# A gated, dilated convolution with fewer products: the next block's first product inside this block's slot, and plain rows moved to the front

## The chip, the cores and the metric

The kernel runs on one core of a Trainium2 chip. The metric is the device time of one execution in microseconds. Instructions run on five engines, each in its own order: TensorE (PE: matmuls; PEld: its weight loads), VectorE (DVE), ScalarE (ACT), GpSimd (POOL) and the sync engine (SP), from which nearly all transfers are issued. They wait for one another through semaphores.

## What is computed

Input x is [2, 16000, 256], w is [3, 256, 512] and w_o is [256, 256], all in bf16. The convolution has three taps, is causal, and has a dilation of two:

```
h[t] = x[t] @ w[0] + x[t-2] @ w[1] + x[t-4] @ w[2]     # 512 columns, zeros ahead of t = 0
z    = tanh(h[:, :256]) * sigmoid(h[:, 256:])
out  = z @ w_o
```

## The kernel before

**Groups.** The 32000 time steps are cut into groups. Fifteen *wide* groups hold 256 rows of 8 consecutive steps each. One of them (the eighth) holds rows of both batches, so its VectorE and GpSimd steps on x are two instructions instead of one. *Plain* groups hold rows of 4 steps: 128 rows at the start (`groups[0]`), 64 rows behind these (`extra`), and 128 rows at the end (`groups[-1]`). x is loaded with a transposing DMA (`load_wide`, L112, and `load_plain`, L98), channels on the 128 partitions; the first plain group is loaded as it is and turned on TensorE.

**Plain blocks.** A group has four blocks, one for each 128 of the 512 columns of h, in the order 0, 2, 1, 3, so that a tanh block is followed by its sigmoid block. A plain block multiplies each of the three taps by x (`direct`, L290 to L307). Tap 1 needs two operands, since its phases come from different rows.

**Wide blocks.** A wide block computes the eight phases with 14 matmuls of 128x512 instead of 24. It needs sums and differences of x, made once per group: `qs` in two halves (`wide_pairs`, "pairs", L217), `qp` (`wide_p`, "p", L223), `qm` in two halves (`wide_m`, "m", L226) and `qd` in two halves (`wide_d`, "d", L236). VectorE makes all of them but one half of `qd`, which GpSimd makes in two slices. Each of these tiles has two buffers, so a group writes into those of two groups back. It also needs six combinations of the weights; two of them, wt and wu, are made on TensorE with identity matrices (`weight_mm`, L171) and copied by ScalarE.

A block B has a PSUM tile `y` of two banks (three buffers; an output pool `o_ps` has two of one bank). Its steps, with T = TensorE, A = ScalarE, V = VectorE, G = GpSimd:

1. `first` (T, 2 matmuls on `qp`) into bank 0; `keep_first` (A, L274) copies it times 4 to `st`
2. `second` (T, 2, on `qm`) adds to bank 0; `keep_second` (A, L278) copies it times 2 to `sv`; `other` (G, L281) makes the other half of `sv` as sv - st
3. `third` (T, 2, on `qm`) adds to bank 0, behind keep_second; `split_bank` (V, L284) makes bank 1 from bank 0 and st
4. `late(B, 0)` (T, 4, on `qs`) adds to both banks, behind split_bank; `rest` (V, L288) subtracts both banks from `sv`; `activate(B, "sv")` (A, L322) gives four phases
5. `late(B, 1)` (T, 4, on `qd`) adds to both banks, behind rest; `activate(B, "y")` (A, L324) gives the other four
6. after two blocks, `gate` (V, L329) multiplies tanh and sigmoid halves; after four, the group's eight *pieces* are projected: `out_mm` (T, 4 matmuls of 128x256, L353), `out_evict` (A, L396), and a store by SP for every two pieces

**The order.** Every engine's order is written out by hand. A *slot* k stands for block k of all (slots 4 to 63 are the wide blocks; a group's slots 0 to 3 are those of its blocks). In the loop before (L496 to L532), with B the slot's block and V the one before it, TensorE does

```
first(B)  late(V, 0)  second(B)  [a block of extra, L518]  two pieces  third(B)  late(V, 1)
```

ScalarE does keep_first(B), "y" of the block before V, keep_second(B), two evictions, "sv" of V. VectorE does the gate that is due (a group's slots 0 and 2), then the steps for the next group (`prep`, L472 to L483: slot 1 pairs and d, slot 2 p, slot 3 pairs and m, next group's slot 0 the second m), then rest(V) and split_bank(B). GpSimd does a slice of `qd` in a group's slots 1 and 3, then other(B), both behind the last of VectorE's steps of this slot (`after`, which keeps GpSimd's reads of SBUF behind VectorE's instructions with two SBUF inputs). The slot of the first wide block (L433 to L450) is written out ahead of the loop, with wt and wu between its products.

Behind the loop (L536 to L577) stand the last wide block's late products, the last plain group, six waiting pieces, and then the last wide group's eight pieces and the plain group's two, evicted by ScalarE and VectorE in turn and stored one by one or in twos.

Of the kernel before, what the change touches and what calls it, by code (L numbers as in the profile page):

```python
# [13 lines left out]
def kernel(  # L14
# [42 lines left out]
    for b in range(B):  # L57
        t, end = (4 * (P + RE) if b == 0 else 0), (T - 4 * P if b == B - 1 else T)
        while t < end:
            n = min(need, (end - t) // 8)  # L60
# [29 lines left out]


# [112 lines left out]
    def wide_new(G):  # L204
        if "q" not in G:
            G["q"] = q_pool.tile([P, 2, 2, 2, CT, RW], bf16, name="qs")
            G["qm"] = q_pool.tile([P, 2, 2, CT, RW], bf16, name="qm")
            G["qp"] = q_pool.tile([P, 2, CT, RW], bf16, name="qp")
            G["qd"] = q_pool.tile([P, 2, 2, CT, RW], bf16, name="qd")

    def wide_pairs(G, h):

        wide_new(G)
        for col, sl in G["cols"]:
# [3 lines left out]
                out=G["q"][:, h, :, :, :, sl].rearrange("p h q ct r -> p h (q ct) r"),  # L218
# [3 lines left out]
    def wide_p(G):  # L222
        return nc.vector.tensor_tensor(out=G["qp"][:], in0=G["q"][:, 0, 0], in1=G["q"][:, 0, 1], op=ALU.subtract)  # L223

    def wide_m(G, h):
        return nc.vector.tensor_tensor(out=G["qm"][:, h], in0=G["q"][:, h, 0], in1=G["q"][:, h, 1], op=ALU.add)  # L226

    def wide_d(G, h, qs, eng, behind=None):

        wide_new(G)  # L230
        j = slice(4 + 2 * h + qs.start, 4 + 2 * h + qs.stop)
        for col, sl in G["cols"]:
# [3 lines left out]
            ins = after(eng.tensor_tensor(out=G["qd"][:, h, qs, :, sl], in0=a, in1=s, op=ALU.subtract), behind)  # L236
# [9 lines left out]
    def mm(B, wmat, mv, bank, first=False):  # L246
        for ct in range(CT):
            nc.tensor.matmul(  # L248
                B.y[:, bank, :], lhsT=wmat[:, ct, B.osl], rhs=mv[:, :, ct, :],
                start=first and ct == 0, stop=ct == CT - 1, skip_group_check=True,  # L250
            )

    def first(B):
        B.y = new_y()
        mm(B, W["wmh"], B.G["qp"], 0, True)
# [34 lines left out]
    def direct(B, taps, out):  # L290

        xt, R = B.G["x"], B.R
        xp, yp, xc, yc = views(B.G)
        for tap in taps:
            if tap == 1:
# [4 lines left out]
            for h, mv in parts:  # L300
                to = out if h is None else out[:, 2 * h * R:2 * (h + 1) * R]
                for ct in range(CT):
                    nc.tensor.matmul(  # L303
                        to, lhsT=w_taps[tap][:, ct, B.osl], rhs=mv[:, :, ct, :],
                        start=tap == TAPS[0] and ct == 0, stop=tap == TAPS[-1] and ct == CT - 1,
# [22 lines left out]
    def gate(G, dts):  # L328
        return nc.vector.tensor_tensor(out=G["z"][:, dts], in0=G["th"][:, dts], in1=G["sg"][:, dts], op=ALU.mult)  # L329
# [46 lines left out]
    def out_evict(G, rb0, jp, on_dve, single=False):  # L376
        o_ps = G["o", rb0, jp]
        copy = nc.vector.tensor_copy if on_dve else nc.scalar.copy
        if jp is None:
# [5 lines left out]
            for j in range(4):  # L385
                nc.sync.dma_start(out=rows[j], in_=osb[(j % 2) * n:(j % 2 + 1) * n, j // 2, :])
# [15 lines left out]
    extras = [Block(extra, oi) for oi in range(4)]  # L402
    ND = 4
    NB = len(blocks) - 4
# [28 lines left out]
    first(blocks[ND])  # L433
    keep_first(blocks[ND])
    for k in range(2, ND):
        activate(blocks[k], bank(blocks[k], k))
    weight_mm("wt")
    second(blocks[ND])
    keep_second(blocks[ND])
    weight_copy("wt")  # L440
    weight_mm("wu")
    weight_copy("wu")
    third(blocks[ND])
    split_bank(blocks[ND])
    wide_d(G0, 0, slice(0, 1), nc.gpsimd, last)
    other(blocks[ND], last)
    wide_d(G0, 0, slice(1, 2), nc.gpsimd, last)
    last = wide_d(G0, 1, slice(0, 2), nc.vector)
    load_wide(loaded_wide)
    loaded_wide += 1  # L450


    todo, made, pend = [], [], []
    gate_at = {}

    def note_gates(B, k):

        if B.oi % 2 == 1:
            gate_at.setdefault(k + 1, []).append((B.G, slice(B.oi // 2, B.oi // 2 + 1)))

    def do_gates(k):
        ins = None
        for G, dts in gate_at.pop(k, []):
            ins = gate(G, dts)
            if dts.stop == NT:
                todo.extend(pieces(G))
        return ins

    gate_at[ND + 1] = [(groups[0], slice(0, 1)), (groups[0], slice(1, 2))]
    gate_at[ND + 5] = [(extra, slice(0, 2))]  # L470

    prep = {}  # L472
    for G in wides[1:]:
        k0 = 4 * G["g"]
        for at, step in (
            (-3, lambda G=G: wide_pairs(G, 0)),
            (-3, lambda G=G: wide_d(G, 1, slice(0, 2), nc.vector)),
            (-2, lambda G=G: wide_p(G)),
            (-1, lambda G=G: wide_pairs(G, 1)),
            (-1, lambda G=G: wide_m(G, 0)),  # L480
            (0, lambda G=G: wide_m(G, 1)),
        ):
            prep.setdefault(k0 + at, []).append(step)  # L483
# [11 lines left out]

    for k in range(ND + 1, NB):  # L496
        B, V = blocks[k], blocks[k - 1]
        first(B)
        keep_first(B)
        late(V, 0)  # L500
        for Y in pend:
            activate(Y, "y")
            note_gates(Y, k)
        last = do_gates(k) or last
        for step in prep.pop(k, []):
            last = step() or last
        rest(V)
        second(B)
        keep_second(B)
# [5 lines left out]
        if k <= ND + 4:  # L515
            E = extras[k - ND - 1]
# [91 lines left out]
```

## Time and profile before

| | |
|---|---|
| time, median of 3 runs (lowest to highest) | 273.63 us (273.53 to 274.45) |
| the profiled execution: its own time | 274.15 us |
| its span, first to last instruction | 272.1 us |
| granted TensorE clock, mean | 0.997 |
| busy: PE, DVE, ACT, POOL | 261.4, 226.6, 248.7, 107.6 us |
| matmuls recorded | 1463 |

The profile shows one execution. Its page gives for each engine the busy time, for groups of instructions their count, mean duration and the idle time ahead of them, and a chain followed back from the last instruction to what released each step. The trace answers finer questions: single instructions in order of time, and who waited for whom. Matmuls are pipelined: a matmul of 512 columns is recorded as 0.38 us long, but the next one starts 0.216 after it, and its recorded end is modelled. On ScalarE and VectorE too, the next instruction may start about 0.1 ahead of the recorded end of the one before. So the texts count from start to start.

### The profile page before, as it was taken

The numbers are of one execution on the slowest core, as the hardware profiler recorded it, in microseconds if no ns is written. First come the engines' busy times: TensorE is split into PE (matmuls) and PEld (weight loads), VectorE is DVE, ScalarE is ACT, GpSimd is POOL, SyncE is SP. The second block draws the span as 40 slices with busy tenths as digits, with TensorE's granted clock in tenths as the row PEclk, the third lists the DMA queues.
The fourth block names the chain that finished last, engine by engine and source line by source line (L and its number), as shares of the span: only waits on it lengthen the run. The fifth ranks groups of instructions, "written<-read, shape, count | busy, mean of one in ns | idle before, by whom it ended". The sixth has DMA issues, their size and how long they took to land.

```text
span 272.1 us, 4200 instructions
## 1 busy us (share of the span) xinstructions
PE 261.4 (96%) x1463; PEld 142.1 (52%) x1464; DVE 226.6 (83%) x260; ACT 248.7 (91%) x380; POOL 107.6 (40%) x100
## 2 busy tenths in 40 slices
PE   7698999999999999999999999999999999999993
PEld 3443545555555555555555555555555555555572
DVE  2877998998898898899889889888988988876634
ACT  3577889999999999999999999999999999999882
POOL 1045355335435533544543453454345345423100
PEclk9999999999999999999999999999999999999998
DMA  8959441471927349192653919264381923122125
GB/s 208 206 116 201 80 94 51 127 192 55 198 106 170 113 109 209 52 223 85 142 143 99 217 42 241 78 150 132 102 215 41 241 79 93 69 77 77 41 77 193
DMA packets 78612, 35.00 MB, mean 129 GB/s; under 512 B 68864, under 2 KB 70912, under 8 KB 78592
## 3 DMA queue, kind: packets, MB, share of 16 engines
q1 hardware_dynamic: 77776, 34.09, 49.5%
q10 hardware_dynamic: 816, 0.66, 0.7%
q8 instruction: 11, 0.18, 0.3%
q14 instruction: 9, 0.07, 0.1%
HBM read 1.18 MB, written 16.38 MB: 65 GB/s over the span
## 4 chain that ended last, share of the span: by engine, by line
PE 86%; DVE 6%; DMA 3%; ACT 2%; issue 1%; SPq 0%; DVEq 0%
PE y L248 64%; PE o_ps L353 18%; DMA xq<-in_x_dram 3%; PE y L303 2%; DVE sv L288 1%; DVE qs L217 1%; PE y L171 1%; DVE y L284 1%; ACT st L274 1%; PE y L353 1%; DVE qd L236 1%; ACT sv L278 1%; ACT thw L324 1%; DVE zw L329 1%; DVE qp L223 1%
## 5 line engine op out<-in xcount | busy, mean ns | idle before, releaser
L281 POOL TENSOR_TENSOR sv<-sv,st 128x512 f32<-128x512 f32 x60 | 76.4, 1274 | 81.2 <-ACT sv L278 75.4
L288 DVE TENSOR_TENSOR sv<-sv,y 128x1024 f32<-128x1024 f32 x60 | 72.6, 1211 | 5.7 <-PE y L248 4.2
L396 ACT CAST osb<-o_ps 128x512 bf16<-128x512 f32 x115 | 63.0, 614 | 1.4 <-PE o_ps L353 1.3
L248 PE MATMUL y<-qd,wd_sb 128*128 128x512 bf16 x240 | 61.5, 379 | 1.3 <-DVE sv L288 1.1
L284 DVE SCALAR_TENSOR_TENSOR y<-st,y 128x512 f32<-128x512 f32 x60 | 41.8, 696 | 24.9 <-PE y L248 24.8
L353 PE MATMUL o_ps<-wo_sb,zw 128*128 128x256 bf16 x464 | 60.3, 273 | 0.0
L236 POOL TENSOR_TENSOR qd<-xq 128x512 bf16<-128x512 bf16 (+2 forms) x32 | 31.5, 988 | 65.1 <-DVE qm L226 39.6
L353 PEld LDWEIGHTS <-zw 128*128 128x128 bf16 x480 | 47.0, 98 | 17.6 <-issue 0.2
L274 ACT ACTIVATE st<-y 128x512 f32<-128x512 f32 x60 | 35.9, 598 | 8.5 <-PE y L248 5.4
L329 DVE TENSOR_TENSOR zw<-thw,sgw 128x2048 bf16<-128x2048 bf16 x30 | 38.7, 1292 | 2.8 <-ACT sgw L324 2.8
L248 PEld LDWEIGHTS <-wd_sb 128*128 128x128 bf16 x240 | 23.2, 97 | 30.3 <-DVE sv L288 1.6
L248 PE MATMUL y<-qp,wmh_sb 128*128 128x512 bf16 x120 | 35.7, 379 | 2.1 <-DVE qp L223 2.1
L217 DVE TENSOR_TENSOR qs<-xq 128x2048 bf16<-128x2048 bf16 (+2 forms) x32 | 36.8, 1154 | 0.8 <-DMA xq<-in_x_dram 0.8
L278 ACT ACTIVATE sv<-y 128x512 f32<-128x512 f32 x60 | 36.2, 603 | 1.4 <-PE y L248 1.4
L248 PE MATMUL y<-qm,w_sb 128*128 128x512 bf16 x120 | 35.5, 377 | 0.7 <-ACT sv L278 0.4
L248 PE MATMUL y<-qs,wt_sb 128*128 128x512 bf16 x120 | 35.7, 379 | 0.4 <-DVE y L284 0.4
L248 PE MATMUL y<-qm,wph_sb 128*128 128x512 bf16 x120 | 35.7, 379 | 0.0
L248 PE MATMUL y<-qs,wu_sb 128*128 128x512 bf16 x120 | 35.7, 379 | 0.0
L322 ACT ACTIVATE thw<-sv 128x1024 bf16<-128x1024 f32 x30 | 32.9, 1096 | 1.2 <-DVE sv L288 1.1
L322 ACT ACTIVATE sgw<-sv 128x1024 bf16<-128x1024 f32 x30 | 32.9, 1097 | 0.1
L324 ACT ACTIVATE sgw<-y 128x1024 bf16<-128x1024 f32 x30 | 30.5, 1017 | 0.6 <-PE y L248 0.6
L324 ACT ACTIVATE thw<-y 128x1024 bf16<-128x1024 f32 x30 | 30.6, 1019 | 0.0
(61 smaller groups left out, 167.6 us busy)
## 6 DMA issues: line engine op xcount, KB each, us to landing
out_dram<-osb SPq DMA_DIRECT2D x57, 256.0 KB, 2.0
out_dram<-osb_end SPq DMA_DIRECT2D x6, 128.0 KB, 1.8
w_sb<-in_w_dram ACTq DMA_DIRECT2D x2, 256.0 KB, 4.4
out_dram<-osb SPq DMA_DIRECT2D x2, 224.0 KB, 2.3
osb<-in_x_dram SPq DMA_DIRECT2D x1, 256.0 KB, 3.0
w_sb<-in_w_dram SPq DMA_DIRECT2D x1, 256.0 KB, 4.5
xq<-in_x_dram SPq DMA_TRANSPOSE x16, 6.9
wo_sb<-in_w_o_dram ACTq DMA_DIRECT2D x1, 128.0 KB, 2.6
```

The costliest lines, as they stand in the source:

```text
L217: ins = nc.vector.tensor_tensor(out=G["q"][:, h, :, :, :, sl].rearrange("p h q ct r -> p h (q ct) r"), in0=s, in1=a, op=ALU.subtract if h ...
L248: nc.tensor.matmul(B.y[:, bank, :], lhsT=wmat[:, ct, B.osl], rhs=mv[:, :, ct, :], start=first and ct == 0, stop=ct == CT - 1, skip_group_c ...
L274: nc.scalar.mul(B.st[:], B.y[:, 0, :], 4.0)
L278: nc.scalar.mul(B.sv[:, 0], B.y[:, 0, :], 2.0)
L281: after(nc.gpsimd.tensor_tensor(out=B.sv[:, 1], in0=B.sv[:, 0], in1=B.st[:], op=ALU.subtract), behind)
L284: nc.vector.scalar_tensor_tensor(out=B.y[:, 1, :], in0=B.st[:], scalar=-0.5, in1=B.y[:, 0, :], op0=ALU.mult, op1=ALU.add)
L288: nc.vector.tensor_tensor(out=B.sv[:], in0=B.sv[:], in1=B.y[:], op=ALU.subtract)
L322: nc.scalar.activation(out=dst[:, 2:4, :], in_=B.sv[:], func=func, scale=0.5)
L324: nc.scalar.activation(out=dst[:, 0:2, :], in_=B.y[:], func=func, scale=0.5)
L329: return nc.vector.tensor_tensor(out=G["z"][:, dts], in0=G["th"][:, dts], in1=G["sg"][:, dts], op=ALU.mult)
L353: nc.tensor.matmul(o_ps[:, q, :], lhsT=z_columns(G, rb0, jp, q, dt), rhs=wo_sb[:, dt, :], start=(dt == 0), stop=(dt == NT - 1),)
L396: copy(out=G["osb"][:, 2 * h:2 * h + 2, :], in_=o_ps)
```

## The change

Five things change.

- **Order in a slot.** The next block N's first product is made in this block's slot, one of its two matmuls ahead of third and one behind it, and keep_first(N) follows. TensorE's order becomes late(V, 0), second(B), two pieces, first(N) matmul 0, third(B), first(N) matmul 1, late(V, 1).
- **Other engines' orders.** VectorE's steps are in two lists, `small` (d, p, m and the gates of the front tiles) done first, and `big` (pairs and gates) behind them. So d comes ahead of pairs, p and m ahead of the gate, and m ahead of pairs. ScalarE's "sv" comes ahead of keep_first(N). GpSimd's slice comes ahead of second(B) in the program. Pieces whose gate is done in a slot are projected from the next slot on.
- **Start.** The first wide block's slot is part of the loop. wt and wu are made on TensorE ahead of its first product.
- **Plain rows.** `extra` has 128 rows instead of 64 and its blocks run in slots 4 to 7, in slots 4 and 5 with two of their taps at the head of the slot; half of its gate is made by GpSimd. One piece instead of two is projected in these slots.
- **End.** The last plain group has 64 rows. Its x is loaded as rows of 8 steps that overlap by 4, so that each tap has one operand (`load_end`), and two blocks share a bank and an activation. The last group's pieces are evicted in twos by ScalarE and VectorE and stored two at a time with one DMA.

The tiles `q`, `qm`, `qp`, `qd` are now taken when they are first written. The diff, cut to its core:

```
-        t, end = (4 * (P + RE) if b == 0 else 0), (T - 4 * P if b == B - 1 else T)
+        t, stop = (4 * 2 * P if b == 0 else 0), (T - 4 * RE if b == B - 1 else T)
...
-    groups.append(dict(wide=False, b=B - 1, r0=T // 4 - P, R=P))
-    extra = dict(wide=False, b=0, r0=P, R=RE, g="e")
+    extra = dict(wide=False, b=0, r0=P, R=P, g="e")
+    end = dict(wide=False, b=B - 1, r0=T // 4 - RE, R=RE, g="z")
...
+    def load_end():
+        xe = end["x"] = xt_pool.tile([P, 8, CT, RE], bf16, name="xe")
+        rows = x[end["b"], 4 * (end["r0"] - 1):4 * (end["r0"] + RE), :].rearrange("(r j) c -> r (j c)", j=4)
+        src = bass.AP(tensor=rows.tensor, offset=rows.offset, ap=[[4 * D, RE], [1, 8 * D]])
+        nc.sync.dma_start_transpose(out=xe[:].rearrange("p j ct r -> p (j ct) r"), in_=src)
...
-    def first(B):
-        B.y = new_y()
-        mm(B, W["wmh"], B.G["qp"], 0, True)
+    def first(B, ct):
+        if ct == 0:
+            B.y = new_y()
+        nc.tensor.matmul(
+            B.y[:, 0, :], lhsT=W["wmh"][:, ct, B.osl], rhs=B.G["qp"][:, :, ct, :],
+            start=ct == 0, stop=ct == CT - 1, skip_group_check=True,
+        )
...
+            if B.G is end:
+                parts = [(None, xt[:, 4 - 2 * tap:8 - 2 * tap])]
...
+    weight_mm("wt")
     for k in range(2):
         activate(blocks[k], bank(blocks[k], k))
...
+    weight_mm("wu")
     for k in range(2, ND):
         activate(blocks[k], bank(blocks[k], k))
...
+    for ct in range(CT):
+        first(blocks[ND], ct)
     weight_copy("wt")
+    keep_first(blocks[ND])
     weight_copy("wu")
...
+    small[ND] = [lambda: wide_d(G0, 1, slice(0, 2), nc.vector)]
+    small[ND + 1] = [lambda: gates_of(groups[0], slice(0, 2))]
+    small[ND + 2] = [lambda: gates_of(extra, slice(0, 1))]
     for G in wides[1:]:
         k0 = 4 * G["g"]
-            (-3, lambda G=G: wide_pairs(G, 0)),
-            (-3, lambda G=G: wide_d(G, 1, slice(0, 2), nc.vector)),
-            (-2, lambda G=G: wide_p(G)),
-            (-1, lambda G=G: wide_pairs(G, 1)),
-            (-1, lambda G=G: wide_m(G, 0)),
-            (0, lambda G=G: wide_m(G, 1)),
+            (-3, big, lambda G=G: wide_pairs(G, 0)),
+            (-3 if G["n"] > 1 else -2, small, lambda G=G: wide_d(G, 1, slice(0, 2), nc.vector)),
+            (-2, small, lambda G=G: wide_p(G)),
+            (-1, big, lambda G=G: wide_pairs(G, 1)),
+            (-1, small, lambda G=G: wide_m(G, 0)),
+            (0, small, lambda G=G: wide_m(G, 1)),
...
+    for k in range(ND, NB):
+        B, V = blocks[k], (blocks[k - 1] if k > ND else None)
+        E, early = (extras[k - ND] if k < ND + 4 else None), k < ND + 2
+        if E:
+            E.y = ps_o.tile([P, BANK], f32, name="e_ps", tag="o_ps")
+            if early:
+                direct(E, TAPS[:2], E.y[:])
+        if V:
+            late(V, 0)
+        if k >= ND + 2:
+            Y = blocks[k - 2]
             activate(Y, "y")
             note_gates(Y, k)
+        last = do(small, k) or last
+        last = do(big, k) or last
+        if k == ND:
+            wide_d(G0, 0, slice(0, 1), nc.gpsimd, last)
+            wide_d(G0, 0, slice(1, 2), nc.gpsimd, last)
         at = (2, 3) if B.G["n"] == 0 else (1, 3)
         if B.oi in at and B.G["n"] + 1 < len(wides):
             q = at.index(B.oi)
             wide_d(wides[B.G["n"] + 1], 0, slice(q, q + 1), nc.gpsimd, last)
+        second(B)
+        keep_second(B)
+        if k == ND + 4:
+            after(gate(extra, slice(1, 2), nc.gpsimd), last)
+            ready.extend(pieces(extra))
         other(B, last)
+        if V:
+            rest(V)
+        if E:
+            direct(E, TAPS[2:] if early else TAPS, E.y[:])
+        project(1 if E else 2)
+        evict()
+        N = blocks[k + 1] if k + 1 < NB else None
+        if N:
+            first(N, 0)
         third(B)
         split_bank(B)
+        if V:
+            activate(V, "sv")
+        if N:
+            first(N, 1)
+            keep_first(N)
+        if E:
+            activate(E, E.y[:])
+        if V:
+            late(V, 1)
+        todo += ready
+        ready.clear()
...
     late(V, 0)
+    activate(Y, "y")
     rest(V)
+    do(big, NB)
+    project(2)
     evict()
+    ye = new_y()
...
     activate(V, "sv")
+    plain_ends(ACT.Tanh, 0)
     late(V, 1)
     activate(V, "y")
+    plain_ends(ACT.Sigmoid, 1)
...
+    gate_phases(slice(2, 4))
...
+    for n, ps in enumerate(left):
+        quad(ps, n % 2 == 1)
+        for i, piece in enumerate(ps):
+            out_evict(*piece, i == 1)
+        if n == 0:
+            gate(end, slice(0, 2))
+            gate_phases(slice(0, 2))
+    for piece in pieces(end):
+        out_mm(*piece)
+        out_evict(*piece, False)
+    todo = [[(G, rb0, jp) for jp in jps] for jps in ((1, 2), (0, 3)) for rb0 in range(0, RW, P)]
+    for n, ps in enumerate(todo):
+        quad(ps, n % 2 == 0)
+        quad_store(ps, nc.sync)
```

`plain_ends` multiplies two end blocks into one bank of `ye` and activates them together. `quad` makes two pieces, into the two banks of a `y` buffer or into two of `o_ps`; `quad_store` evicts one with ScalarE and one with VectorE and issues one store for both. `gate_phases` makes the last gate for half of the phases at a time.

More of the change, by code (lines that the diff above doesn't have):

```diff
@@ L402 @@
     extras = [Block(extra, oi) for oi in range(4)]
+    ends = [Block(end, oi) for oi in range(4)]
     ND = 4
-    NB = len(blocks) - 4
+    NB = len(blocks)
     def bank(B, i):
@@ L445, with do, gates_of @@
[L445 to L454, printed above, removed]
+    ready, todo, made = [], [], []
+    small, big = {}, {}
+    def do(steps, k):
+        ins = None
+        for step in steps.pop(k, []):
+            ins = step() or ins
+        return ins
+    def gates_of(G, dts):
+        if dts.stop == NT:
+            ready.extend(pieces(G))
+        return gate(G, dts)
@@ L456, in note_gates @@
     def note_gates(B, k):
         if B.oi % 2 == 1:
[L459 to L472, printed above, removed]
+            big.setdefault(k + 1, []).append(lambda: gates_of(B.G, slice(B.oi // 2, B.oi // 2 + 1)))
@@ L530 @@
                 loaded_wide += 1
[L531 to L546 removed]
+            elif "x" not in end:
+                load_end()
+    assert not small
+    Y, V = blocks[NB - 2:]
```

153 lines of the change are left out of this document (60 added, 93 removed).

## The prediction

> **What bounds the kernel now.** I read the page's first part, then its chain, then the chain in order of time, then the timeline of one slot. Columns of the first: busy us, share of the span, instructions.
>
> ```profile
> span 272.1 us, 4200 instructions
> PE 261.4 (96%) x1463; PEld 142.1 (52%) x1464; DVE 226.6 (83%) x260; ACT 248.7 (91%) x380; POOL 107.6 (40%) x100
> PE 86%; DVE 6%; DMA 3%; ACT 2%; issue 1%; SPq 0%; DVEq 0%
> ```
>
> TensorE is busy throughout, and 86% of the chain that ends last is its work. This work has to be done in any case; only its waits can go. The chain in order of time (start, length) repeats one pattern per slot:
>
> ```profile
> 125.12 0.87 PE o_ps L353 x8
> 125.99 3.10 PE y L248 x14
> ...
> 252.37 0.87 PE o_ps L353 x8
> ```
>
> From 125.12 to 252.37 are 32 slots, 3.977 us each. Whether TensorE waits in them the timeline shows (start, length, engine, line; brackets: idle before and its releaser):
>
> ```profile
> 141.16 0.60 ACT L278 ACTIVATE sv<-y 128x512 f32<-128x512 f32 x1
> 141.64 1.09 ACT L396 CAST osb<-o_ps 128x512 bf16<-128x512 f32 x2
> 141.82 0.59 PE L248 MATMUL y<-qm,w_sb 128*128 128x512 bf16 x2
> 142.04 1.28 POOL L281 TENSOR_TENSOR sv<-sv,st 128x512 f32<-128x512 f32 x1
> 142.58 1.10 ACT L322 ACTIVATE thw<-sv 128x1024 bf16<-128x1024 f32 x1
> 143.11 0.59 PE L248 MATMUL y<-qp,wmh_sb 128*128 128x512 bf16 x2
> 143.12 1.28 DVE L329 TENSOR_TENSOR zw<-thw,sgw 128x2048 bf16<-128x2048 bf16 x1
> 143.74 0.60 ACT L274 ACTIVATE st<-y 128x512 f32<-128x512 f32 x1
> 144.24 1.02 ACT L324 ACTIVATE thw<-y 128x1024 bf16<-128x1024 f32 x1
> 144.32 0.68 DVE L226 TENSOR_TENSOR qm<-qs 128x1024 bf16<-128x1024 bf16 x1
> 144.84 1.04 PE L353 MATMUL o_ps<-wo_sb,zw 128*128 128x256 bf16 x8
> 144.93 1.21 DVE L288 TENSOR_TENSOR sv<-sv,y 128x1024 f32<-128x1024 f32 x1
> 145.14 0.60 ACT L278 ACTIVATE sv<-y 128x512 f32<-128x512 f32 x1
> 145.79 0.59 PE L248 MATMUL y<-qm,w_sb 128*128 128x512 bf16 x2
> ```
>
> From the third product (141.82) to the projection (144.84) are 14 matmuls in 3.02 us, 0.2157 each; the projection's eight take 0.87 (chain). TensorE alone would need 3.89 us. The next third (145.79) starts 0.08 late: it waits for keep_second (L278, ends 145.74), which stands behind the "y" activation (L324) and keep_first (L274), which waited for the first product (143.11 + 0.59 = 143.70). So a ring closes in 3.97 us: first 0.59 + 0.04, keep_first 0.50, "y" 0.90, keep_second 0.60 + 0.05, third and late 1.29. **The ring sets the slot, 0.085 above TensorE's own work.** Over slots 11 to 63 that is 53 x 0.085 = 4.5 us, with 0.3 more where a group spans both batches: 4.8.
>
> TensorE's other waits lie in front:
>
> ```profile
> 5.11 5.40 PE L303 MATMUL y<-xt,w_sb 128*128 128x512 bf16 x32 [0.44 <-ACT xt L188]
> 12.56 0.61 PE L248 MATMUL y<-qp,wmh_sb 128*128 128x512 bf16 x2 [2.05 <-DVE qp L223]
> 17.57 0.59 PE L248 MATMUL y<-qs,wt_sb 128*128 128x512 bf16 x2 [0.42 <-DVE y L284]
> 22.34 1.04 PE L248 MATMUL y<-qd,wd_sb 128*128 128x512 bf16 x4 [1.14 <-DVE sv L288]
> 24.94 0.83 PE L303 MATMUL e_ps<-xte,w_sb 128*128 128x256 bf16 x8
> 25.90 0.59 PE L248 MATMUL y<-qm,w_sb 128*128 128x512 bf16 x2
> ```
>
> A bracket starts at a matmul's modelled end, 0.16 after its slot is free, so idle is bracket plus 0.16: 2.2, 0.58, 1.30. The e_ps group frees its slot at 25.60 (24.94 + 0.83 - 0.17) and third follows 0.3 later, behind keep_second; three times. With 0.9 of smaller ones up to 43 us: 5.9. All waits: about 10.8 (4.8, 5.9, and 0.1 at the end).
>
> **The change part by part.** Blocks, tiles and columns multiplied are the same: 64 plain rows move from the end to the front. So I compare TensorE's waits, and what follows its last product.
>
> *The slot.* Let T be the start of the second half of a first product (ct 1). New order: late(V,1) T+0.22 (ends 1.24), late(.,0) 1.08, second 1.94 (ends 2.53), projection 2.37, half a first 3.24, third 3.46, next T at 3.89. keep_second starts at 2.57 and ends at 3.17: third has 0.24 to spare, the ring is open. ScalarE's steps, start to start: keep_first 0.50, "y" 0.90, keep_second 0.48 (141.16 to 141.64), two evictions 0.94 (to 142.58), "sv" 0.96 where nothing holds the next one:
>
> ```profile
> 253.93 1.10 ACT L322 ACTIVATE thw<-sv 128x1024 bf16<-128x1024 f32 x1
> 254.89 1.06 ACT L324 ACTIVATE thw<-y 128x1024 bf16<-128x1024 f32 x1
> ```
>
> Sum 3.78 of 3.89: it keeps up, with 0.11 spare. This gains 0.085 where nothing else comes late. **Next in line is VectorE.** Its steps, and GpSimd's:
>
> ```profile
> 131.19 1.22 DVE L217 TENSOR_TENSOR qs<-xq 128x2048 bf16<-128x2048 bf16 x1
> 132.33 0.69 DVE L236 TENSOR_TENSOR qd<-xq 128x1024 bf16<-128x1024 bf16 x1
> 133.10 1.04 POOL L236 TENSOR_TENSOR qd<-xq 128x512 bf16<-128x512 bf16 x1 [1.86 <-DVE qd L236]
> 134.09 1.28 POOL L281 TENSOR_TENSOR sv<-sv,st 128x512 f32<-128x512 f32 x1
> ```
>
> Pairs (L217) cost 1.14 start to start, a gate 1.20 (143.12 to 144.32), m (144.32 to 144.93) 0.61, and so p and d (L236), of its size. split_bank follows third at T+0.20 and leaves VectorE free at T+0.80. Then come the slot's steps, and rest (1.21 until its end), for which late(V,1) waits at T+4.11. In a group's slots 0, 2 and 3 the steps are 1.75 to 1.81: rest ends at 3.82, 0.24 before late needs it. In a group's slot 1 the change puts d ahead of the pairs, where it stood behind them. d writes the qd buffer of two groups back (two buffers), which the late(V,1) of the last block of that group reads until T+1.24. So d starts at 1.28, pairs 1.89, rest 3.03 to 4.24, late(V,1) 4.29: **TensorE waits 0.18**, with ScalarE's "sv" behind the same rest.
>
> GpSimd's slice of qd follows the pairs and moves with them: 3.16 to 4.20, then other (0.99 after the slice's start) 4.15 to 5.42. In the group's slot 2 p wants to start at 4.76 and meets it. What that costs:
>
> ```profile
> 38.39 1.28 POOL L281 TENSOR_TENSOR sv<-sv,st 128x512 f32<-128x512 f32 x1
> 39.14 1.61 DVE L329 TENSOR_TENSOR zw<-thw,sgw 128x2048 bf16<-128x2048 bf16 x1
> ```
>
> Pairs of the same size, not overlapped, took 1.22. The gate at 143.12 overlapped GpSimd's other (142.04 + 1.28) by 0.20 and took 1.28; the one at 39.14 overlapped it by 0.53 and took 1.61. VectorE stands while GpSimd works, but for some 0.14. So p counts from 5.28, gate 5.89, rest 7.09 to 8.30; late(V,1), which TensorE reaches at 8.18, waits to 8.35: 0.17. I take 0.15, as slices and gates differ by a few hundredths. In the Trainium skill, "SBUF — State Buffer" (section Who interferes with whom) says that a VectorE instruction with two SBUF inputs and a GpSimd one that reads SBUF block each other fully; the two gates agree, save the 0.14.
>
> Of the 13 groups with d first, 12 lie in slots 11 to 63: 12 x 0.33 + 0.3 at the batch border = 4.3 us of waits, against 4.8. **Gain 0.5: the ring's gain is nearly all given back.**
>
> *Front.* The 12 matmuls of wt and wu (2.59 us) now run right behind the first group's 32, from 10.31, while VectorE makes qp (ready at 12.50): the wait of 2.2 is gone. If that cover failed (a PSUM buffer not free), 2.2 would be back. New waits, placed by the same rows: third of the first wide block behind the copy of wu 0.3, the next third behind its keep_second 0.2; that block's late(V,1) 1.35, because d follows qp, pairs and two m (12.4 + 1.14 + 3 x 0.61 = 15.4), then GpSimd makes two slices (to 17.4) and other (to 18.7) with gate and pairs held behind them, so rest ends at 21.2 where TensorE is ready at 19.9. Slots 8 and 10 have no projection, as pieces now wait for the next slot; TensorE's own work there is 3.02, ScalarE's 3.78 - 0.94 + 0.5 for a front tile's activation = 3.3, the old ring 3.97: bounds 0.3 and 0.95 each. Placed in order, with ScalarE late from the slots before, I get 0.9 and 0.65. Small ones 0.35. Sum 3.75 against 5.9: **gain 2.15**. The front plain tile grows from 80 to 144 rows, and holds the sync queue longer ahead of the second wide load:
>
> ```profile
> 8.29 1.27 SPq L98 DMA_TRANSPOSE xte<-in_x_dram  x1
> 19.34 1.22 DVE L217 TENSOR_TENSOR qs<-xq 128x2048 bf16<-128x2048 bf16 x1
> ```
>
> By rows 1.27 becomes 2.3 us. The pairs at 19.34 show no DMA wait; with my 18.8 for them, a wait up to 0.5 would be hidden by GpSimd's hold. One gate of the front tile moves to GpSimd, whose gates no row shows: bounds are nothing and 1.3 (other's size); I take the slice's 1.04, which lies inside slot 8's wait.
>
> *Tail.* Only half as much plain work covers the last activations. late(.,0) stands behind split_bank with no first between them: 0.1. The first leftover pair of pieces ends 1.04 after its start; VectorE evicts (0.61, a copy being as long as m) and makes the end tile's gate (half an m, 0.35 to 0.4): at 2.15 the end piece may start, and TensorE is there after two pairs, 1.75: 0.4. Before, 0.1: **loss 0.4**. One operand per tap makes fewer, wider matmuls of the same columns: bounds minus 0.1 and 0.1, taken as nothing. Behind TensorE's last product:
>
> ```profile
> 266.87 1.04 PE L353 MATMUL o_ps<-wo_sb,z 128*128 128x256 bf16 x8
> 268.30 0.68 DVE L390 CAST osb_end<-o_ps 128x512 bf16<-128x512 f32 x1
> 268.87 0.89 SPq L363 DMA_DIRECT2D out_dram<-osb_end  x2
> ```
>
> TensorE ends at 267.9, the last copy at 268.98, and the last of two stores in a row goes out some 0.4 later. The copies now lag as long (a pair in the y buffers before it holds VectorE up), but one store of both pieces leaves at once; its landing may be slower for twice the size. Between nothing and 0.4, taken as half: **gain 0.2.**
>
> Sum: 0.5 + 2.15 - 0.4 + 0.2 = 2.45, say 2.5. The profiled execution had a span of 272.1 and took 274.15; the median of the runs is 273.63, 0.5 less. The span goes to 269.6, the median to **271.1 us**.
>
> **The rivals.**
> 1. *d does not wait* (the earlier reader of qd is through when VectorE gets there). Then all slots run at 3.89 and 12 x 0.33 = 4.0 more is gained: 267.1. For it: all four slots fit on paper. Against: late(V,1) ends 0.44 after VectorE is free. Chance 0.20.
> 2. *Third still waits for keep_second*: ScalarE has 0.11 to spare per slot, and one late step closes the ring again. Then the 29 slots without a VectorE wait stay at 3.977: 2.5 more, 273.6, no change. Chance 0.12.
> 3. *Slower: GpSimd becomes the ring*, in each group's slots 2 and 0. In slot 3 the slice (2.67) and other (3.66 to 4.93) already end 0.24 past the next m; with the 0.14 this holds it 0.10, inside its spare 0.24. From 0.14 more on, each tenth costs TensorE a tenth in slot 0, and slot 2 pays it in full. If VectorE's instructions hold GpSimd in turn by the 0.27 between slice and other lengths, (0.27 - 0.14) + 0.27 = 0.40 per group, 4.8 in all: 275.9. Against: GpSimd's rows keep 1.04 and 1.28 when overlapped. Chance 0.10.
> 4. *VectorE stands for the whole overlap*, without the 0.14: 12 x 0.14 = 1.7 more, 272.8, no change. The two gates speak against it. Chance 0.06. This is what the page "SBUF — State Buffer" of the Trainium skill would give.
>
> **How the numbers follow.** The forecast has 0.52, with its own range 269.9 to 272.2 (waits of 0.05 a slot either way in the 24 slots that wait). A measurement of this kernel can tell about 0.5% from no change, 1.4 us: faster means under 272.3. Faster: 0.52 less 0.01, and 0.20: 0.71. Within: 0.12 + 0.06 + 0.01 = 0.19. Slower: 0.10. Eight in ten: from 266.5 (most of rival 1) to 273.8 (rival 4 and over half of rival 2).
>
> **What would show it.** Slots 0 and 3 of a group 3.89 apart, slots 1 and 2 about 0.15 longer. Among VectorE's waits, qd behind TensorE's y, 13 times, near 0.47; among TensorE's, y behind VectorE's sv some two dozen times. keep_second no longer ends a TensorE wait past slot 11. No wait for qp near 12.5. I am wrong if VectorE's d shows no wait (rival 1), if third still starts 0.05 after keep_second's end (rival 2), or if other ends over 0.3 past the next small step in slot 0 (rival 3).

## The result and the profile after

The kernel takes **275.06 us** (median of 6 runs, 274.83 to 276.01); the kernel before beside it 273.83 (273.53 to 274.45). The ratio is **1.0051** (95% interval 1.0032 to 1.0070): slower by half a per cent, where 271.1 us and "faster" were forecast. The same kernel run again with the last experiments gave 1.0037 (1.0024 to 1.0050). The profiled execution took 275.64 with a span of 273.6.

The page's first lines and its chain, as shown of before (busy us, share, instructions):

```profile
span 273.6 us, 4186 instructions
PE 262.9 (96%) x1456; PEld 142.7 (52%) x1456; DVE 232.2 (85%) x260; ACT 249.0 (91%) x377; POOL 108.6 (40%) x101
PE 89%; DVE 3%; ACT 2%; issue 1%; DMA 1%; DVEq 0%
```

TensorE's share of the chain rose and the time rose too, so these lines don't say where the time went. The chain in order of time does. Here are the projections of one group and a half:

```profile
126.41 0.87 PE o_ps L365 x8
...
130.30 0.87 PE o_ps L365 x8
...
134.20 0.87 PE o_ps L365 x8
...
138.28 0.87 PE o_ps L365 x8
...
142.37 0.87 PE o_ps L365 x8
...
146.26 0.87 PE o_ps L365 x8
```

The even 3.977 us of before have become 3.89, 3.90, 4.08, 4.09, 3.89. Inside the two long slots the timeline shows, in order, d, the pairs, rest, p, the gate and rest again, with GpSimd's two pieces among them:

```profile
132.94 0.70 DVE L241 TENSOR_TENSOR qd<-xq 128x1024 bf16<-128x1024 bf16 x1 [0.31 <-PE y L253]
133.56 1.22 DVE L223 TENSOR_TENSOR q<-xq 128x2048 bf16<-128x2048 bf16 x1
...
134.69 1.21 DVE L297 TENSOR_TENSOR sv<-sv,y 128x1024 f32<-128x1024 f32 x1
...
134.91 1.04 POOL L241 TENSOR_TENSOR qd<-xq 128x512 bf16<-128x512 bf16 x1 [2.51 <-PE o_ps L365]
...
135.56 0.38 PE L261 MATMUL y<-qp,wmh_sb 128*128 128x512 bf16 x1
...
135.91 1.27 POOL L290 TENSOR_TENSOR sv<-sv,st 128x512 f32<-128x512 f32 x1
...
135.96 1.02 PE L253 MATMUL y<-qd,wd_sb 128*128 128x512 bf16 x4
...
136.43 1.30 DVE L229 TENSOR_TENSOR qp<-q 128x1024 bf16<-128x1024 bf16 x1
...
138.79 1.21 DVE L297 TENSOR_TENSOR sv<-sv,y 128x1024 f32<-128x1024 f32 x1
...
139.63 0.38 PE L261 MATMUL y<-qp,wmh_sb 128*128 128x512 bf16 x1
...
140.05 1.02 PE L253 MATMUL y<-qd,wd_sb 128*128 128x512 bf16 x4
```

In the first of them d waits 0.31 for TensorE (its bracket), rest ends at 135.90, and the late products start at 135.96. The matmul ahead of them (135.56) freed its slot 0.216 later, so TensorE lost 0.18. In the next slot p (136.43) takes 1.30 instead of 0.69, beside GpSimd's other; rest ends at 140.00, late starts at 140.05, and TensorE lost 0.20.

The end is the other place. TensorE's last rows, the last copy, and the sync queue:

```profile
266.48 1.04 PE L365 MATMUL o_ps<-wo_sb,zw 128*128 128x256 bf16 x8
...
267.90 0.68 DVE L604 CAST osb_end<-o_ps 128x512 bf16<-128x512 f32 x1
```

```profile
265.01 1.27 SPq L398 DMA_DIRECT2D out_dram<-osb_odd  x2
266.38 3.30 SPq L612 DMA_DIRECT2D out_dram<-osb_end  x4
```

TensorE ends 0.4 us earlier than before and the last copy as well, yet the span is 1.5 longer. The page's DMA part has the first trace of the reason: the end's stores (`osb_end`) land 4.1 us after their issue, where those of before, of half the size, took 1.8. Of the end piece's stores (`osb_odd`, the piece of the 64-row group, which has no partner) the page gives no landing. The first line is of after, the other three of before:

```profile
out_dram<-osb_end SPq DMA_DIRECT2D x4, 256.0 KB, 4.1
```

```profile
out_dram<-osb_end SPq DMA_DIRECT2D x6, 128.0 KB, 1.8
out_dram<-osb_odd SPq DMA_DIRECT2D x4, 32.0 KB, 1.9
38.28 2.47 SPq L386 DMA_DIRECT2D out_dram<-osb_odd  x4
```

In the kernel before, the odd piece belonged to `extra`, in front, and left at 38.28 in four stores of 32 KB. The change gives the 64 rows to the end group, so the odd piece is now stored at 265.01, right ahead of the last four stores. It also rewrites these stores, an edit that the diff above leaves out:

```diff
-for j in range(4):
-    nc.sync.dma_start(out=rows[j], in_=osb[(j % 2) * n:(j % 2 + 1) * n, j // 2, :])
+for q in range(2):
+    nc.sync.dma_start(out=rows[2 * q:2 * q + 2], in_=osb[:, q, :])
```

Each store of before wrote one phase and had the 64 rows as its outermost dimension. Each store of after writes two phases, and these two are its outermost dimension.

I cut both profiled spans, and a second one of the changed kernel, into stretches, and took from each the columns that its matmuls have, at 0.2157 us for 512 (the forecast's figure). What is left is TensorE's waiting, and slower products where it had them. The profile of before has records of 11 of the 12 matmuls of wt and wu; all 12 are counted. Each cell: length, and what is left.

| stretch | before | after | after, again |
|---|---|---|---|
| start to first plain product | 5.11 | 5.38 | 5.38 |
| to third product of slot 10 | 36.94, 6.3 | 37.61, 4.6 | 37.08, 4.1 |
| to third product of slot 63 | 211.12, 5.3 | 211.45, 5.9 | 211.46, 5.9 |
| to the end of the last product's slot | 14.58, 0.35 | 12.91, 0.83 | 12.91, 0.83 |
| to the end of the span | 4.37 | 6.23 | 6.23 |
| span | 272.1 | 273.6 | 273.1 |

Front and tail came near the forecast. The slots lost 0.55 instead of gaining 0.5, and the last stretch lost 1.86 instead of gaining 0.2.

### The profile page after: what moved, and what is told of

It is laid out like the page before. It is cut to its first block, busy times and chain, and to the rows that moved or that the text cites. A ratio compares the mean times of both kernels' runs of the same rounds, so it can differ in the third digit from the quotient of the medians.

```text
span 273.6 us, 4186 instructions
## 1 busy us (share of the span) xinstructions
PE 262.9 (96%) x1456; PEld 142.7 (52%) x1456; DVE 232.2 (85%) x260; ACT 249.0 (91%) x377; POOL 108.6 (40%) x101
## 4 chain that ended last, share of the span: by engine, by line
PE 89%; DVE 3%; ACT 2%; issue 1%; DMA 1%; DVEq 0%
PE y L253 55%; PE o_ps L365 18%; PE y L261 9%; PE y L315 4%; PE e_ps L315 1%; DVE sv L297 1%; DMA osb<-in_x_dram 1%; PE y L178 1%; DVE qp L229 1%; PE y L365 1%; DVE y L293 1%; ACT sv L287 0%; ACT st L283 0%; ACT thw L334 0%; ACT wu_sb L184 0%
## 5 line engine op out<-in xcount | busy, mean ns | idle before, releaser
L409 ACT CAST osb<-o_ps 128x512 bf16<-128x512 f32 x113 | 60.6, 592 | 1.6 <-PE o_ps L365 1.6
L365 PE MATMUL o_ps<-wo_sb,zw 128*128 128x256 bf16 x456 | 59.1, 273 | 0.0
L261 PE MATMUL y<-qp,wmh_sb 128*128 128x512 bf16 x120 | 45.3, 379 | 0.7 <-ACT thw L336 0.7
L223 DVE TENSOR_TENSOR q<-xq 128x2048 bf16<-128x2048 bf16 (+2 forms) x32 | 36.7, 1152 | 1.3 <-DMA xq<-in_x_dram 1.3
L253 PE MATMUL y<-q,wu_sb 128*128 128x512 bf16 x120 | 35.7, 379 | 0.0
L253 PE MATMUL y<-q,wt_sb 128*128 128x512 bf16 x120 | 35.7, 379 | 0.0
L341 DVE TENSOR_TENSOR zw<-thw,sgw 128x2048 bf16<-128x2048 bf16 x29 | 35.2, 1215 | 0.0
L334 ACT ACTIVATE sgw<-sv 128x1024 bf16<-128x1024 f32 x30 | 32.0, 1068 | 2.8 <-DVE sv L297 1.7
L334 ACT ACTIVATE thw<-sv 128x1024 bf16<-128x1024 f32 x30 | 32.1, 1069 | 2.0 <-DVE sv L297 1.0
```

The costliest lines, as they stand in the source:

```text
L223: ins = nc.vector.tensor_tensor(out=sums(G, "q")[:, h, :, :, :, sl].rearrange("p h q ct r -> p h (q ct) r"), in0=s, in1=a, op=ALU.subtract ...
L253: nc.tensor.matmul(B.y[:, bank, :], lhsT=wmat[:, ct, B.osl], rhs=mv[:, :, ct, :], start=False, stop=ct == CT - 1, skip_group_check=True,)
L261: nc.tensor.matmul(B.y[:, 0, :], lhsT=W["wmh"][:, ct, B.osl], rhs=B.G["qp"][:, :, ct, :], start=ct == 0, stop=ct == CT - 1, skip_group_che ...
L334: nc.scalar.activation(out=dst[:, 2:4, :], in_=B.sv[:], func=func, scale=0.5)
L365: nc.tensor.matmul(o_ps[:, q, :], lhsT=z_columns(G, rb0, jp, q, dt), rhs=wo_sb[:, dt, :], start=(dt == 0), stop=(dt == NT - 1),)
L409: copy(out=G["osb"][:, 2 * h:2 * h + 2, :], in_=o_ps)
```

## The experiments

Theory: in the slots d's wait for TensorE makes both long slots, one directly and one by way of GpSimd; at the end, the end piece's two stores hold up the four behind them. Rivals are with each run. "Ratio" is to the kernel before, run on the same chip, with its 95% interval; the kernels before there had medians of 274.2 to 274.3 us.

### The end piece's stores

Run one gives the two stores 64 rows as outermost dimension, by writing the activations with the phase innermost:

```diff
-    out=dst[:].rearrange("p h j r -> p (h j r)"), in_=ye[:, i, :NT * 4 * RE], ...
+    out=dst[:].rearrange("p h j r -> p (h j r)").rearrange("p (a r j) -> p a j r", r=RE, j=2),
+    in_=ye[:, i, :NT * 4 * RE].rearrange("p (a j r) -> p a j r", j=2, r=RE), ...
...
-rows = out[...].rearrange("(r j) d -> j r d", j=4)
+rows = out[...].rearrange("(r j) d -> r j d", j=4)
...
-    nc.sync.dma_start(out=rows[2 * q:2 * q + 2], in_=osb[:, q, :])
+    nc.sync.dma_start(out=rows[:, 2 * q:2 * q + 2], in_=osb[:, q, :])
```

> The changed kernel with the 64-row end piece's output rows laid so that each of its two 64 KB stores has 64 rows as its outermost dimension instead of two; same bytes, same queue, same number of stores. Theory (the two stores are carried by two of the 16 DMA engines, 128 packets of 512 bytes each at 27 ns, which is 3.5 us on those two, and the last four stores wait for these two engines): the last store lands about 2.0 us after its issue instead of 4.1, the end comes 2.0 us earlier, about 273.0 us against 275.06. Rival (256 KB stores in two halves of a row land late by themselves, or SP's issues are late): no change, 275.1 within 0.3.

Measured: 273.66 us, ratio **0.9975** (0.9966 to 0.9984), 0.6 to 0.8% less than the changed kernel: 1.7 to 2.1 us. The stretches of the tail, first of the changed kernel, then of this run (columns: length, busy time of each engine, granted clock, share of the 16 DMA engines, GB/s):

```profile
266.20:268.40 2.20, 1.31 (x13) 0.93 (x10) 1.74 (x4) 1.07 (x2) 0.00 (x0) 1.00 0.17 39
268.40:269.70 1.30, 0.00 (x0) 0.00 (x0) 0.18 (x1) 0.00 (x0) 0.00 (x0) 1.00 0.99 347
269.70:271.50 1.80, 0.00 (x0) 0.00 (x0) 0.00 (x0) 0.00 (x0) 0.00 (x0) 1.00 0.96 337
271.50:272.40 0.90, 0.00 (x0) 0.00 (x0) 0.00 (x0) 0.00 (x0) 0.00 (x0) 0.92 0.12 41
```

```profile
266.20:268.40 2.20, 1.49 (x14) 1.08 (x12) 1.74 (x4) 1.07 (x2) 0.00 (x0) 1.00 0.61 209
268.40:269.70 1.30, 0.00 (x0) 0.00 (x0) 0.36 (x1) 0.00 (x0) 0.00 (x0) 1.00 0.93 317
269.70:271.50 1.80, 0.00 (x0) 0.00 (x0) 0.00 (x0) 0.00 (x0) 0.00 (x0) 1.00 0.56 188
```

In the changed kernel 39 GB/s flow for 2.2 us with a share of 0.17 of the 16 engines, though two 256 KB stores have been issued (266.38 and 266.94). Then all flow for 3.1 us, and for 0.8 us more only 0.12 of the engines, two of them. The packet records say the same. In the changed kernel the 256 packets of 512 bytes run from 266.30 to 269.64 at 29 ns each, so 2.2 engines carry them; by the count those two carry 128 such packets each ahead of their share of the rest. In this run the packets run from 266.50 to 267.49, on 7.0 engines by the mean, with a pause between the two stores, and on 13 in the densest 0.2 us. The landing of the last stores falls from 4.1 to 2.3:

```profile
out_dram<-osb_end SPq DMA_DIRECT2D x4, 256.0 KB, 2.3
```

Theory confirmed. The Trainium skill, "DMA: Bandwidth & Descriptors" (section Why a DMA increments its semaphore by 16 and not by 1), gives the rule: a DMA runs on the largest number of engines up to 16 that divides the slowest dimension of both its patterns. The trace agrees: a dimension of two gave 2.2 engines by the count of packets. For 64 rows the rule gives 16, and the densest 0.2 us had 13.

Run two leaves the rows and moves the issue:

```diff
-    nc.sync.dma_start(out=rows[2 * q:2 * q + 2], in_=osb[:, q, :])
+    nc.scalar.dma_start(out=rows[2 * q:2 * q + 2], in_=osb[:, q, :])
```

> The changed kernel with the end piece's two 64 KB stores issued by ScalarE instead of SP, rows as before. Theory of two DMA engines: no gain, 275.1, or up to 0.7 us more because ScalarE's issues stand ahead of its last copies. Rival (the stores stand ahead of the last four in SP's own queue): the last four no longer wait, landing falls from 4.1 to about 2.0 us, 273.0 us.

Measured: 275.05 us, ratio **1.0025** (1.0016 to 1.0035). Set against the changed kernel's two ratios, that is 0.3 to 0.7 us less, but the intervals overlap, so no gain can be told, as the theory of two engines has it. The rival's 273.0 is out. The last four stores landed after 2.8 us instead of 4.1, but they were also issued later (267.28 to 269.67; in the changed kernel 266.38 to 269.68). ScalarE's part of the tail shows why:

```profile
264.20 1.70 ACTq L398 DMA_DIRECT2D out_dram<-osb_odd  x2
265.94 0.59 ACT L604 CAST osb_end<-y 128x512 bf16<-128x512 f32 x1 [1.77 <-PE o_ps L365]
```

Two issues held ScalarE 1.7 us, its next copy waited 1.77 behind them (the bracket names TensorE, whose product was done by then), and TensorE's tail grew from 12.91 to 14.37. This later end cost the span nothing, because the two engines set the end. The small packets still sat on 2.2 engines, from 265.71 to 269.11. The last packet of all ended at 271.78, 2.67 us after the last small one; in the changed kernel that is 272.30 and 269.64, 2.67 again. (An estimate from the packet records: a sixteenth of the last four stores is 16 packets of 85 ns and 32 of 46 ns, 2.8 us.) So the end follows the small packets, whichever queue they come from.

One thing does differ with the queue. On SP's own queue no packet of the 256 KB stores moves before 268.03, 1.2 us after the first of their issues was over, on any of the engines; here the first moves 0.5 us after. Why the other fourteen engines stand still on the shared queue is not shown. They end before the two do, so it didn't set the time.

### The two long slots

Run three puts d behind the pairs:

```diff
-    (-3 if G["n"] > 1 else -2, small, lambda G=G: wide_d(...)),
+    (-3 if G["n"] > 1 else -2, big if G["n"] > 1 else small, lambda G=G: wide_d(...)),
```

> The changed kernel with VectorE's difference d behind the pair sums in a group's slot 1 (the order of the kernel before) instead of ahead of them. The prediction's theory: only that slot gets shorter, from 4.08 to 3.89 us, while the next keeps its 4.09 from GpSimd's hold on VectorE's sum p: 13 times 0.19, so 2.5 us, 272.6 us. Rival one (both long slots hang on d): 5.0 us, 270.1 us. Rival two (d only stands where some other wait would: ScalarE's or VectorE's pace sets the slots): 275.1 us, no change.

Measured: 270.41 us, ratio **0.9860** (0.9847 to 0.9873), 4.9 to 5.2 us less than the changed kernel. My expectation missed; rival one had it. All four slots of a group are 3.895 long, but for one of 4.15 at the group that spans both batches. Its chain:

```profile
131.89 0.87 PE o_ps L365 x8
...
135.78 0.87 PE o_ps L365 x8
...
139.68 0.87 PE o_ps L365 x8
...
143.57 0.87 PE o_ps L365 x8
```

and the slot in which p had been held, where other now ends at 134.40:

```profile
133.13 1.27 POOL L290 TENSOR_TENSOR sv<-sv,st 128x512 f32<-128x512 f32 x1
...
134.12 0.83 DVE L229 TENSOR_TENSOR qp<-q 128x1024 bf16<-128x1024 bf16 x1
```

p overlaps other by 0.28 and takes 0.14 more than its 0.69. The hold itself is as forecast (overlap less 0.14; in the changed kernel overlap 0.75, excess 0.61). What my expectation forgot is in the prediction: the pairs move with d, GpSimd's slice with the pairs, and other with the slice. Is it d's wait or its place? Run four leaves the place and takes away the earlier reader, with a third buffer:

```diff
-G[nm] = q_pool.tile(SUMS[nm], bf16, name=nm)
+G[nm] = q_pool.tile(SUMS[nm], bf16, name=nm, bufs=3 if nm == "qd" else 2)
```

> The changed kernel, d ahead of the pairs as it is, but with three buffers for d's output instead of two, so that d has no earlier reader to wait for. Theory (d waits for TensorE's last reading of its buffer, and pairs, rest, GpSimd's slice and the next slot's p come late behind it): no wait of d for TensorE in the trace, all slots 3.895 us, as with d behind the pairs: 4.6 to 5.2 us less than the changed kernel, ratio to the kernel before 0.986 to 0.989. Rival (not the wait but the order: d's 0.61 us ahead of the pairs makes GpSimd's slice late): the long slots keep half of their 0.18 us or more, ratio 0.995 or above.

Measured: 270.50 us, ratio **0.9864** (0.9847 to 0.9881), slots of 3.895, and no wait of d for TensorE. In the changed kernel it stands among VectorE's waits (total us, times, longest):

```profile
DVE qd L241 <- PE y L253: 4.1, 13, 0.3
```

So it is the wait, and not the place. Run five keeps it, and takes GpSimd's slice out of the slot where it makes other late:

```diff
-at = (2, 3) if B.G["n"] == 0 else (1, 3)
+at = (2, 3)
```

> The changed kernel with GpSimd's first slice of a group moved from slot 1 to slot 2, d's order and buffers as they are. Theory (in slot 2 it is GpSimd's late work that holds VectorE's p: 1.30 us instead of 0.69): p takes 0.7, slot 2 falls from 4.07 to 3.90 us, slot 1 stays at 4.07: 2.3 us less than the changed kernel, ratio to the kernel before 0.996 to 0.998. Rival (VectorE is late in slot 2 from slot 1's wait whatever GpSimd does): both stay, ratio 1.005. Second rival (the slice in slot 2 only moves the hold to slot 3): slot 3 becomes longer by up to 0.18, ratio 1.005.

Measured: 272.29 us, ratio **0.9931** (0.9915 to 0.9947), some 3 us less than the changed kernel, where 2.3 was expected. Slot 1 keeps its 4.08, slot 2 falls from 4.09 to 3.895, and two of the slots 0 grow, to 4.00 and 4.16. The stretch of slots is 208.94 long against 211.46: 2.5 of the 3 us. p is back at its size:

```profile
133.30 1.28 POOL L290 TENSOR_TENSOR sv<-sv,st 128x512 f32<-128x512 f32 x1 [2.88 <-ACT sv L287]
...
134.71 0.68 DVE L229 TENSOR_TENSOR qp<-q 128x1024 bf16<-128x1024 bf16 x1
```

Theory confirmed: GpSimd's late other makes slot 2, d's wait slot 1, and the first exists only because of the second.

Run six asks whether the new place of the first product opened the ring. It takes run three and moves first and keep_first back:

```diff
-if N:
-    first(N, 0)
 third(B)
...
-if N:
-    first(N, 1)
-    keep_first(N)
...
 if V:
     late(V, 1)
+if N:
+    for ct in range(CT):
+        first(N, ct)
+    keep_first(N)
```

> The changed kernel with d behind the pairs (270.4 us), and with the next block's first product and its keep_first moved back behind the block's last products, as in the kernel before. Theory (the new place of the first product opens the ring from keep_first over the y activation and keep_second to the third product): the ring closes again, slots 3.977 us instead of 3.895, third waits for keep_second: 53 times 0.082 = 4.3 us more, 274.8, ratio to the kernel before about 1.002. Rival (the slots are short for another reason, such as GpSimd or VectorE work moved by the change): 270.4 stays, ratio 0.986.

Measured: 276.17 us, ratio **1.0071** (1.0055 to 1.0087), 5.8 us more than run three. The ring is closed again: means of 3.985 to 4.001, most slots 3.977. keep_second ends at 155.77 and third follows 0.04 later:

```profile
155.16 0.61 ACT L287 ACTIVATE sv<-y 128x512 f32<-128x512 f32 x1
...
155.81 0.59 PE L253 MATMUL y<-qm,w_sb 128*128 128x512 bf16 x2
```

So the new place of the first product is what opened the ring. The 53 slots lost 4.8 us where 4.3 was expected, and the rest of the 5.8 came ahead of them. The half us more lies in single slots of 4.0 to 4.2; their reason stays open.

### The start

In the profile of the changed kernel the first plain products came at half speed. The group of 32 took 7.36 us (before, 5.40):

```profile
5.38 7.36 PE L315 MATMUL y<-xt,w_sb 128*128 128x512 bf16 x32 [0.34 <-ACT xt L195]
...
15.16 0.59 PE L261 MATMUL y<-qp,wmh_sb 128*128 128x512 bf16 x2
```

One by one, the records have 427 ns between starts until 9.2 us, then 216. The granted clock of the stretch doesn't show it (first column after GpSimd's is the clock, 1.00):

```profile
4.00:13.00 9.00, 8.65 (x42) 4.61 (x43) 6.07 (x8) 4.80 (x8) 0.00 (x0) 1.00 1.08 228
```

Run seven fills the gaps ahead of them:

```diff
-    for n in range(8):
+    for n in range(9):
...
+    blocks[0].y = new_y()
+    for n in range(2):
+        nc.tensor.matmul(blocks[0].y[:, 0, :256], lhsT=warm[:, :P], rhs=warm[:, :256], start=True, stop=True)
     for taps in (TAPS[:1], TAPS[1:2], TAPS[2:]):
```

> The changed kernel with one more 512-column warm-up product before the first input lands, and two of 256 columns between the transposes and the first plain products. Theory (TensorE's clock in the first 9 us depends on the idle gaps that fall in one stretch of activity, and by chance on when a run starts): the plain products' spacing of 427 ns until 9.4 us goes, 216 from the start, in every run: median 0.5 us less, 274.6, and less spread than 1.2 us. Rival one (the changed kernel always starts cold): 1.0 us less, 274.1. Rival two (the gaps aren't the reason): no change, and the profile again shows 427 ns until 9 us.

Measured: 274.95 us, ratio **1.0032** (1.0019 to 1.0044), not to be told from the changed kernel's 1.0037 and 1.0051. The products are quick from the second or third on, and the group behind them starts 2 us earlier. Two thirds of that are gone by slot 10:

```profile
5.12 5.65 PE L315 MATMUL y<-xt,w_sb 128*128 128x512 bf16 x32
...
13.20 0.59 PE L261 MATMUL y<-qp,wmh_sb 128*128 128x512 bf16 x2
...
21.59 1.02 PE L253 MATMUL y<-qd,wd_sb 128*128 128x512 bf16 x4 [1.25 <-DVE sv L297]
```

TensorE reaches the first wide block's late products early and waits 1.25 us there for VectorE's rest (bracket). With the slow start it arrives when rest is done. The third product of slot 10 comes at 42.31 instead of 42.99. Three more runs:

> The changed kernel once more, unaltered, beside the others on one chip. 1.005 of the kernel before, 275.1 to 275.7 us. If the plain products' clock at the start is chance, this profile may show them at 216 ns from the start (then the tenth slot's third product comes near 42.4 us, as in the runs with a quick start) or at 427 ns up to 9 us (near 43.0); if the change itself made it cold, always 427 ns.

Measured: ratio 1.0037 (1.0024 to 1.0050). Its plain products were slow again, until about 8 us, and the third product of slot 10 came at 42.46.

> The kernel before with the same longer warm-up (one more 512-column product ahead of the input, two of 256 behind the transposes). If the start's clock is chance in both kernels, its median falls by as much as the changed kernel's did, 0.5 us, ratio 0.998, and its profile shows 216 ns from the start. If only the changed kernel starts cold, no change, ratio 1.000.

Measured: 274.12 us, ratio **0.9994** (0.9981 to 1.0007): no difference. The interval ends next to the first number of the expectation and holds the second, so this run's time hardly tells them apart. The profiles say a little more: the three with the longer warm-up reached full pace early (their twelfth product came at 7.3 to 8.1 us), and of ten without it two did (7.5; the others 8.7 to 10.1). That the gaps are the reason is likely by this, and not shown. The change doesn't force the slow start: of the two quick ones one is the kernel before, the other the changed kernel with its stores on ScalarE. "TensorE: Matmul & The Clock Gate" of the Trainium skill (Part 1: The HAM clock gate) describes a clock that is halved until TensorE was busy through a window of 3.4 us that runs freely. Spacings of 427 and 216 ns, and a switch at unlike times, agree with it; no run here shows the window itself.

### Together

> The changed kernel with d behind the pairs and the end piece's stores spread over 64 rows, the warm-up as it was. If both costs add: 0.986 - 0.0075 = 0.9785 of the kernel before, 268.3 us; with the longer warm-up as well it was 0.9799, so a longer warm-up would then gain nothing in this kernel. If the warm-up is worth its 0.5 us here too: 0.9815, 269.2 us.

Measured: 269.13 us, ratio **0.9807** (0.9783 to 0.9831). The interval holds both numbers of the expectation. With the longer warm-up as well:

> The changed kernel with d behind the pairs, the end piece's stores spread over 64 rows, and the longer warm-up together. If the three costs are separate they add: d behind the pairs took off 5.2 us, the spread 2.0, the warm-up 0.5: 0.986 - 0.0075 - 0.002 = 0.9765 of the kernel before, about 267.9 us. If one hides behind another (the stores only show because TensorE is late, or the warm-up is absorbed by the front's waits): between 268.5 and 270.4.

Measured: 268.77 us, ratio **0.9799** (0.9780 to 0.9817). The sum of all three, 0.9765, is outside the interval. The two costs nearly add (run one saved 0.0069 against the mean of 1.0037 and 1.0051, and 0.9860 less that is 0.979); the warm-up adds nothing that can be told. This is the best version: 2% below the kernel before.

## Why the prediction was wrong

*The store behind the last product* is the step that failed. It said "gain 0.2": copies lag as long, and one store leaves for both pieces. It priced the last four stores and left out the two of the end piece, which the change puts right ahead of them and writes in a form that two DMA engines carry. The runs showed a loss of 1.86 there instead, 2.1 of the 3.5 us by which forecast and second profile differ (-2.5 against +1.0). Run one, which changes the form alone, takes the stretch from 6.23 to 4.56: 1.7 of the 2.1 are the form. The rest is the step as it was reasoned: with the form put right 4.4 us follow TensorE's modelled end where before 4.2 did, so 0.2 was lost even there, not gained.

*The slot* had the right mechanism and two mis-sized terms. The ring is open: no wait of third for keep_second past slot 11, and run six closes it. What is left over TensorE's columns in the 53 slots is 5.3 us before, 5.9 after, and 1.3 with d behind the pairs. So the ring was worth 4.1 where 4.5 was put: 0.082 in each of 52 slots, as TensorE's own slot is 3.895 and not 3.89, less 0.18 by which slot 10 grew. The waits that begin with d cost 4.6 where 4.0 was put: 0.18 and 0.19 in each of 12 groups, not 0.18 and 0.15, and a little more at the batch border and in slot 10. (The forecast's 4.8 and 4.3 both hold 0.3 for the border, which stays in all three kernels.) A gain of 0.5, the difference of two large terms, so became a loss of 0.55. That is 1.05 of the miss.

Of its signs, the spacing of the slots came as forecast, and so did the 13 waits of d, though at 0.31 and not near 0.47. The two dozen waits of y for sv are not in the list of TensorE's waits, which has three. Such a wait is 0.18 to 0.20 long and its bracket opens only 0.16 after the slot is free; the spacing shows them all.

*Rival 1* (d does not wait) was refuted as it stood, and runs three and four show that its price was nearly right: 4.0 forecast, 4.6 there in the slots. *Rival 2* fell with the ring. *Rival 3*: slot 0 kept its 3.895, so GpSimd's other didn't set it. *Rival 4*: the 0.14 stands, twice more. The slower result came by a way that none of them named.

*Front*: gain 2.15 forecast, 1.7 and 2.2 measured, the lower one with the slower start. The wait for qp is gone, and the wait of late forecast at 1.35 shows as 1.25 where the start was quick. *Tail*: loss 0.4 forecast, 0.48 measured; the end piece waits for its gate (bracket, 0.24 after the modelled end):

```profile
263.41 0.61 PE L365 MATMUL o_ps<-wo_sb,z 128*128 128x256 bf16 x4 [0.24 <-DVE z L341]
```

What is left of the difference is 0.27 us from the start to the first plain product; the first input landed 3.2 us after its issue instead of 3.0.

## What to carry to other kernels

When work moves to the end of a kernel, look at its stores too: at what is queued behind them, and at the outermost dimension of their patterns. Here two small stores on two engines, ahead of the last ones, cost 1.7 us, and a shape with 64 rows outermost took that back. A forecast that is the small difference of two large terms has the errors of both: here a gain of 0.5 was 0.01 us per slot. An instruction with little work placed first in a queue is dear when its buffer's last reader is late: place it where it need not wait, or give it another buffer.

## What the runs showed of the hardware

Two 64 KB stores with two as their outermost dimension ran together at 39 GB/s on 2.2 engines for 3.3 us; the same bytes with 64 rows outermost took 1.0 us. The kernel's last packet came 2.67 us after the last packet of the slow stores, whether SP or ScalarE had issued them. VectorE's p, which has two SBUF inputs, was longer beside GpSimd's work, by the overlap less 0.14 us (overlap 0.75 and 0.28, excess 0.61 and 0.14). TensorE's products may come at half pace (427 ns for 512 columns) up to 9 us into one profile and nearly not at all in another with the same front, while the granted clock of the stretch reads 1.00. And 2 us lost in front were worth 0.7 us at slot 10.
